# A linear-attention and maxout-FFN kernel: another hand-made order for its 1478 steps

## The chip, the cores and the metric

The kernel runs on one core of a Trainium2 chip. The metric is the device time in microseconds of one execution; the time of the kernel before is the median of three runs. The five engines are called as the profile calls them: PE (matrix products), DVE (vector), ACT (activation), POOL (GpSimd) and SP (here a queue of DMA issues alone).

## The reference

```python
def phi(x):                                   # x: 8 x 8 x 576 x 64, w_phi: 64 x 128
    proj = np.einsum('bhsd,df->bhsf', x, w_phi)
    proj = proj - np.max(np.abs(proj), axis=-1, keepdims=True)
    return np.concatenate([np.exp(proj), np.exp(-proj)], axis=-1)
q_p, k_p = (phi(q), phi(k))
kv = np.einsum('bhsf,bhsd->bhfd', k_p, v)
z = np.sum(k_p, axis=2)
num = np.einsum('bhsf,bhfd->bhsd', q_p, kv)
den = np.einsum('bhsf,bhf->bhs', q_p, z)[..., None] + 1e-06
x = (num / den).transpose(0, 2, 1, 3).reshape(4608, 512)
h = np.maximum(np.maximum(x @ w1, x @ w2), x @ w3)   # w1..w3: 512 x 768
out = h @ w_out                                      # 768 x 512, out: 4608 x 512, float32
```

So there are 64 heads of linear attention, and behind them a feed-forward network (FFN) with a maximum of three branches over 4608 tokens.

## The kernel before

**Attention** goes in 16 units of four heads (two units to a batch). A unit loads Q, K and V; casts Q and K to bf16; transposes them (on PE with `tps` for units 0 to 3, with a DMA transpose on SP for the others); projects them (`psq`, `psk`, line 536); takes the maxima on DVE (`mqp`, `mk`, 555); takes the exponentials of K on ACT (`Ek`, 549); turns the maxima of Q and puts them into the transposed Q (`mT`, 567 and 571); projects Q again with the maxima taken off (`psm`, 615) and takes its exponentials (`Eq`, 628); weights V on POOL (`vab`, 590); forms K'V on PE (`kvps`, 644, copied to `kv_sb`, 649); and multiplies (`psn`, 662: four groups of ten products to a unit). DVE divides (`rden`, `x_sb`, 668 and 669), and the result goes transposed into `xT`: over PE for units 0 and 1 (`pxT`, 682), with a DMA transpose on SP for the others (692). This last transfer is called X.

**The FFN** goes in nine chunks of 512 tokens. Chunk 0 to 7 is the first 512 tokens of a batch and needs X of two units; chunk 8 is the 64 last tokens of all batches, put together by POOL (`x_last`, 832). A chunk has 12 products `up` of four matmuls each (`ups`, 715), taken up by ACT or DVE (`hT`, 721 to 725), and then four output tiles: a "straight" product of four matmuls (742), a "down" product of six onto it (747), a copy (`osb`, 755) and two stores (762). The branches are computed as differences to the first one, whose own part is the straight product; for that the weights are combined once at the start (`hT` copies at 802, `pm`, 813). The last tile of chunk 8 is cut into pieces of 256, 128 and 128 columns.

In the first matmuls of an `up`, two read the channels of the even unit and two those of the odd one.

**Order.** Every step is a closure ("node") with a number. A table `PLAN` lists all 1478 of them; each word gives the node, the engine (T for PE, D, A, G for POOL, S for SP), the buffer slots and a start, and `plan` takes them in that order:

```python
n, slots = nodes[int(what[:at])], iter(what[at + 1:])
n.eng, n.start = {"T": "PE", "D": "DVE", "A": "ACT", "G": "POOL", "S": "SP"}[what[at]], float(start)
for b in n.bufs:
    if b.index is None:
        b.index = int(next(slots), 36)
order.append(n)
```

The starts are planned values and no measurement. An engine carries out its instructions in the order in which they come, and waits where an operand or a buffer is not ready. `fill` puts spare matmuls (`idler`, 844) where the table leaves PE idle for long. Weights are loaded on POOL's queue (422), Q, K and V of most units on SP's (475). V of units 1 to 3 is held back by a copy of one element on DVE, the gate (473): the load waits until the copy has written into its buffer.

Of the kernel before, what the change touches and what calls it, by code (L numbers as in the profile page):

```python
# [96 lines left out]
0G@0.72 10S0@0.73 2D0@0.85 3D@1.07 6S0@1.19 1G@1.29 4A@1.30 8S@1.65 86G0@1.79 13S@2.11 15S1@2.57 85G@2.64 1076G@3.49 12D1@3.63  # L97
159G2@4.29 7A@4.38 9A@5.12 158G@5.14 16T1@5.15 5D@5.55 1079G@5.99 17D0@6.25 22T002300@7.02 27T45@7.26 25D@7.51 29A@7.74 26D@8.11
14A@8.45 31D@8.72 24A@9.07 18T6@9.22 23A@9.58 20T7@9.67 19D@9.92 228G1@10.03 28A@10.07 30D@10.54 37T12@10.69 32T36@10.92
21D@11.14 39A@11.17 93T5@11.25 40D@11.37 42T47@11.52 33A@11.66 45D@11.97 91T1@12.12 44A@12.15 35D@12.31 34A@12.49 89T4@12.57  # L100
94D1@12.92 38A@12.98 61T30@13.07 90D@13.27 43A@13.47 64T5@13.55 63A@13.81 92D@13.89 66A@14.30 46D@14.51 95T114111@14.66
65A@14.80 36D@14.85 47A0@15.29 1090T7@15.32 41D@15.46 62A@15.54 50G0@15.69 1086T5@15.92 48G@15.97 98D@16.06 1091A0@16.17
105T62@16.61 1087D@16.77 110T30@16.85 49G@17.09 51A@17.12 58T4@17.18 112A@17.37 113D@17.38 1088T7@17.66 59A@17.91 108D@17.99
52G@18.20 67T5@18.26 111A@18.39 1089D@18.59 162T3@18.74 60A@18.88 164T6@19.19 114D@19.20 53G@19.32 68A@19.37 55T7@19.64
69A@19.73 165D2@19.89 54A@20.07 115T04@20.21 57A@20.37 119D@20.58 70T056@20.66 56A@20.87 118D@20.92 87D0@21.26 117A@21.36
163D@21.36 88S@21.51 183T000700@21.70 116A@21.72 361S1@21.97 109D@21.98 71A@22.06 166T3@22.13 362S1@22.43 184A@22.46 167D@22.59
100T45@22.61 72D@22.81 124A1@22.95 77T30@22.96 104D@23.19 107A@23.20 127G1@23.35 1094T6@23.44 227G@23.63 97A@23.69 103D@23.80
106A@24.18 78D0@24.40 185A@24.67 1098T4@24.74 99D@25.02 102A@25.16 187D@25.63 1095A@25.65 131T21@26.04 96A@26.15 126G@26.16
160D2@26.24 186D@26.34 161S@26.49 173T37@26.62 133A@26.77 168T61@26.85 176D@27.10 1092T0@27.18 101A@27.26 125G@27.28 177D@27.71
120A@27.75 169A@28.00 1099D@28.32 123G@28.40 128T3@28.48 132A@28.49 122G@28.68 229D3@28.93 79T5@28.96 175A@28.97 171D@29.03  # L110
75T4@29.28 170A@29.46 1096T2@29.60 80D1@29.63 121G@29.79 174A@29.95 76D0@30.25 129A@30.44 172D@30.87 73T6@30.90 1077G@30.91
130A@30.95 137T5@31.22 1093A@31.43 1097D@31.48 365G0@31.71 143T141@31.80 138A@31.95 74D1@32.09 139A@32.46 1078G@32.83
188T73@32.84 178T02@32.96 145A@33.09 192D@33.21 140T6@33.28 144A@33.49 231T5@33.52 182D@33.55 364G@33.63 141A@33.89 134T1@33.97
181D@34.15 196A0@34.30 81T4@34.45 142A@34.55 197G0@34.75 191D@34.76 135A@34.89 148T61@35.04 232D0@35.10 152T0@35.36 189A@35.38
146T7@35.68 136A@35.72 149D0@35.72 83T5@36.00 180A@36.20 147D1@36.34 150T1@36.35 82A@36.69 198G@36.84 151D0@36.96 190A@37.34
153D1@37.58 233T6@37.66 179A@37.68 154T7@38.11 199A@38.17 84A@38.32 234D@38.36 193T4@38.42 156T1@38.48 242T110311@38.89
# [759 lines left out]
```

## Time and profile before

| what | value |
|---|---|
| median of three runs | 285.19 us (284.92 to 285.64) |
| the profiled execution's own time | 284.83 us |
| its span in the profile | 283.0 us (1.8 us lie around it) |
| clock of PE granted | 1.00 |
| PE busy | 273.1 us, 96% |
| DVE, ACT, POOL busy | 74%, 69%, 42% |
| first `up` of chunk 0 | at 41.58 us |
| DMA | 51.45 MB, mean 182 GB/s |

Times in rows of the profile are microseconds from the start of the span. In a timeline row stand start, duration of the group, engine, line, operation, output and inputs, count, and in square brackets the idle time of the engine ahead of it with what ended it ("issue": nothing that the profile shows). In a row of waits stand the engine and line, what was waited for, the sum, the count and the longest. In the chain stand start, length and what. In a row of windows stand the window, its length, the busy time of PE, PE's weight loads, DVE, ACT and POOL with their counts, the granted clock, the share of the DMA engines and GB/s.

### The profile page before, as it was taken

The page shows a single profiled execution, that of the slowest core. Times are in us where ns is not written, and L with a number is a line of the kernel's source. Part 1 is how long each engine was busy: PE and PEld are TensorE (multiplying, and loading weights), DVE is VectorE, ACT ScalarE, POOL GpSimd, SP SyncE. Part 2 cuts the span into 40 slices and gives each one's busy share as a digit, 9 for nine tenths or more (in the row PEclk, how much of TensorE's full clock was granted, in tenths as well). Part 3 has the DMA queues.
Part 4 walks back from the last instruction along what each step waited for, and adds up shares of the span by engine and source line. Part 5 has one row for each costly group of instructions (what it writes and reads, how often), then busy time and mean ns, then how long its engine had stood idle before and what let it go on. Part 6 is the DMA issues. An engine that isn't in the chain of part 4 may idle for free.

```text
span 283.0 us, 8534 instructions
## 1 busy us (share of the span) xinstructions
PE 273.1 (96%) x3524; PEld 154.1 (54%) x3563; DVE 208.9 (74%) x441; ACT 195.4 (69%) x447; POOL 117.8 (42%) x107
## 2 busy tenths in 40 slices
PE   8899989999999989999999999999999999999995
PEld 3476764565556635665556465555555455444443
DVE  4799988999887978879879759995886664055232
ACT  2799988898888869897886798887634762230120
POOL 8064787856390836722638609051114600000000
PEclk9999999999999999999999999999999999999999
DMA  7999999999989999999998469969706106050164
GB/s 185 245 207 237 255 172 270 315 213 192 357 328 194 201 271 325 163 241 211 245 299 150 94 188 249 182 123 206 205 1 123 41 2 130 0 109 5 37 145 155
DMA packets 68337, 51.45 MB, mean 182 GB/s; under 512 B 48778, under 2 KB 53066, under 8 KB 68298
## 3 DMA queue, kind: packets, MB, share of 16 engines
q1 hardware_dynamic: 63534, 45.28, 67.5%
q0 software_dynamic: 4000, 4.92, 10.2%
q10 hardware_dynamic: 764, 0.71, 0.7%
q8 instruction: 28, 0.46, 0.6%
q14 instruction: 11, 0.09, 0.1%
HBM read 34.64 MB, written 9.44 MB: 156 GB/s over the span
## 4 chain that ended last, share of the span: by engine, by line
PE 83%; DMA 9%; DVE 5%; issue 1%; POOL 1%; ACT 1%; POOLq 0%
PE ups L715 33%; PE ops L747 14%; PE ops L742 10%; PE psn L662 7%; DMA xT<-x_sb 5%; PE kvps L644 5%; PE psm L615 5%; PE psq L536 5%; DMA qk_bf<-in_q_dram 3%; PE pm L813 2%; DVE mqp L555 1%; DVE mk L555 1%; PE tps L498 1%; DVE qkT L501 1%; DVE x_sb L669 1%
## 5 line engine op out<-in xcount | busy, mean ns | idle before, releaser
L715 PE MATMUL ups<-xT,w_bf 128*128 128x512 bf16 x416 | 100.3, 379 | 2.1 <-DMA xT<-x_sb 1.2
L549 ACT ACTIVATE Ek<-psk 128x512 bf16<-128x512 f32 (+1 forms) x160 | 82.8, 571 | 16.8 <-PE psk L536 13.5
L628 ACT ACTIVATE Eq<-psm 128x512 bf16<-128x512 f32 (+1 forms) x160 | 78.8, 570 | 11.4 <-PE psm L615 10.7
L590 POOL TENSOR_TENSOR vab<-v_raw,em 128x1152 bf16<-128x1152 f32 (+1 forms) x36 | 68.0, 1906 | 44.4 <-ACT em L586 31.7
L715 PEld LDWEIGHTS <-w_bf 128*128 128x128 bf16 x432 | 40.6, 98 | 47.7 <-issue 2.3
L555 DVE TENSOR_REDUCE mqp<-psq 128x4 bf16<-128x512 f32 (+1 forms) x80 | 48.9, 632 | 8.3 <-PE psk L536 6.7
L555 DVE TENSOR_REDUCE mk<-psk 128x4 f32<-128x512 f32 (+1 forms) x80 | 49.0, 628 | 2.9 <-ACT Ek L549 2.1
L747 PE MATMUL ops<-wout_bf,hT 128*128 128x512 bf16 (+2 forms) x216 | 49.3, 367 | 0.6 <-issue 0.2
L721 DVE TENSOR_TENSOR hT<-hT,ups 128x512 bf16<-128x512 bf16 x54 | 36.0, 683 | 16.9 <-PE ups L715 15.2
L747 PEld LDWEIGHTS <-hT 128*128 128x128 bf16 x228 | 21.2, 98 | 22.0
L669 DVE TENSOR_TENSOR x_sb<-psn,rden 128x320 bf16<-128x320 f32 x64 | 31.5, 492 | 2.2
L723 ACT ACTIVATE hT<-ups 128x512 bf16<-128x512 f32 x33 | 19.4, 601 | 19.4 <-PE ups L715 19.3
L662 PEld LDWEIGHTS <-Eq 128*128 128x128 bf16 x640 | 25.2, 97 | 7.8
L725 DVE TENSOR_SCALAR hT<-ups 128x512 bf16<-128x512 f32 x21 | 14.3, 687 | 19.7 <-PE ups L715 19.5
L755 ACT COPY osb<-ops 128x512 f32<-128x512 f32 (+2 forms) x20 | 11.0, 553 | 25.6 <-PE ops L747 15.4
L662 PE MATMUL psn<-kv_sb,Eq 128*128 128x65 bf16 x640 | 27.2, 194 | 0.1
L536 PE MATMUL psq<-w,qkT 64*128 64x128 bf16 x288 | 24.3, 217 | 0.5 <-DVE qkT L501 0.5
L742 PE MATMUL ops<-xT 128*128 128x512 bf16 x88 | 23.9, 380 | 0.4
L536 PE MATMUL psk<-w,qkT 64*128 64x128 bf16 x288 | 24.1, 217 | 0.0
L536 PEld LDWEIGHTS <-qkT 64*128 64x128 bf16 x576 | 16.5, 94 | 12.5 <-issue 9.6
L481 POOL CAST qk_bf<-k_raw 128x1152 bf16<-128x1152 f32 x12 | 13.8, 1146 | 19.9 <-DMA k_raw<-in_k_dram 9.1
L615 PE MATMUL psm<-qkT,wphi_m 128*128 128x512 bf16 (+1 forms) x70 | 21.5, 358 | 0.0
(75 smaller groups left out, 235.7 us busy)
## 6 DMA issues: line engine op xcount, KB each, us to landing
v_raw<-in_v_dram SPq DMA_DIRECT2D x16, 576.0 KB
out_dram<-osb SPq DMA_DIRECT2D x65, 128.0 KB
q_raw<-in_q_dram SPq DMA_DIRECT2D x12, 576.0 KB
k_raw<-in_k_dram SPq DMA_DIRECT2D x12, 576.0 KB
w_bf<-in_moe_w_dram POOLq DMA_DIRECT2D x3, 768.0 KB, 8.2
qk_bf<-in_k_dram POOLq DMA_DIRECT2D x3, 288.0 KB, 13.2
qk_bf<-in_q_dram POOLq DMA_DIRECT2D x3, 288.0 KB, 9.5
wout_bf<-in_moe_w_out_dram POOLq DMA_DIRECT2D x1, 768.0 KB, 17.0
```

The lines of the kernel that those rows point to most:

```text
L536: nc.tensor.matmul(ps()[:, i, :], lhsT=cols[r, :], rhs=w2[r, c, :], start=True, stop=True)
L549: nc.scalar.activation(Ek[s]()[:, tiles_of(t0, n), :], of(1), EXP, scale=1.0 - 2.0 * s)
L555: nc.vector.tensor_reduce((mq, mk)[c]()[:, tiles_of(t0, n)], of(c), AXX, ALU.max, apply_absolute_value=True)
L590: (nc.vector if n_.eng == "DVE" else nc.gpsimd).tensor_tensor(vab()[:, g, t0:t1, 0:D], vb()[:, t0:t1, :], em()[:, g, t0:t1].unsqueeze(2).t ...
L615: nc.tensor.matmul(psm()[:, 0:w], lhsT=wphi_m, rhs=rhs, start=True, stop=True)
L628: nc.scalar.activation(Eqb()[s][:, cols], psm()[:, 0:w], EXP, scale=1.0 - 2.0 * s)
L662: nc.tensor.matmul(psn()[:, c, :], lhsT=Eqb()[g][:, t0:t0 + P], rhs=kv()[:, pr, ab, g, :], start=(g == 0), stop=(g == 1))
L669: nc.vector.tensor_tensor(x_sb()[:, pr, :, ab, :], psn()[:, :, 0:D], rden().to_broadcast([P, 5, D]), ALU.mult)
L715: nc.tensor.matmul(ups(), lhsT=w_bf[i + 1][:, ct, j * P:(j + 1) * P], rhs=tokens_of(ct), start=(ct == 0), stop=(ct == CT - 1))
L721: nc.vector.tensor_tensor(hT()[:, j, :], hT()[:, j, :], ups(), ALU.max)
L742: nc.tensor.matmul(ops_()[:, 0:width], lhsT=tile_of(ct, tt), rhs=line_w[c_i > MOVE][:, ct, cols], start=(ct == 0), stop=False)
L747: nc.tensor.matmul(ops_()[:, 0:width], lhsT=hT()[:, j, tt * P:(tt + 1) * P], rhs=wout_bf[:, j, cols], start=False, stop=(j == JT - 1))
```

## The change

Another `PLAN`, with the same 1478 nodes. Buffers, stages and all other code stay. 84 nodes go to another engine (most are copies out of PSUM between DVE and ACT), the others only to another place or slot. There are 7128 PE rows and 27 idlers in both. The table has 154 lines now, 155 before, so each later line of code has a number lower by one.

```diff
 PLAN = """
...
-353D0@92.97 439A@92.98 419T5@93.35 458A0@93.47 581D@93.59 1171T@93.67 360S@93.74 459A@93.74 420D1@94.19 579A@94.44 576D@94.81
-438A@94.93 1178T1@94.97 754G2@95.02 425S@95.24 1172A3@95.42 575D@95.42 567T75@95.93 578A@96.03 624G1@96.14 562T43@96.17
...
+352T6@92.10 1168A0@92.20 420D1@92.29 577T112511@92.51 572T14@92.75 353D0@92.91 425S@93.06 354T7@93.07 463G@93.11 573A@93.23
+689G2@93.39 1170T3@93.39 355D1@93.64 574A@93.74 579A@94.23 1171T@94.26 576D@94.38 461G@94.51 360S@94.56 578A@94.74 581D@95.38
...
 """
```

Here node 425, X of unit 5, stands behind node 360, X of unit 4, in the old rows and ahead of it in the new ones.

Three places. First PE at the end of attention: `psn` is the last group of unit 15, whose result SP then transposes, `ops` are output tiles of chunk 6, and `ups` is the first `up` of chunk 7. Before:

```order
L662 MATMUL psn_5299<-kv_sb_5224,Eq1_1_78 128x65
...
L742 MATMUL ops_5315<-w0_bf_81,xT_85 128x512 [waits DVE_49]
...
L747 MATMUL ops_5315<-wout_bf_84,hT_4986 128x512
...
L747 MATMUL ops_5280<-wout_bf_84,hT_4986 128x512
...
L742 MATMUL ops_5338<-w0_bf_81,xT_85 128x512
...
L747 MATMUL ops_5338<-wout_bf_84,hT_4986 128x512
...
L715 LDWEIGHTS w1_bf_82 [waits DMAHW1_49,DVE_49]
L715 MATMUL ups_5352<-xT_85,w1_bf_82 128x512 [waits PE_49]
...
L715 MATMUL ups_5352<-xT_85,w1_bf_82 128x512 [waits DMAHW4_49]
```

and now, again from the last `psn` of the unit:

```order
L661 MATMUL psn_5310<-kv_sb_5236,Eq1_0_76 128x65
...
L741 MATMUL ops_5321<-w0_bf_81,xT_85 128x512
...
L746 MATMUL ops_5119<-wout_bf_84,hT_4988 128x512
...
L746 MATMUL ops_5321<-wout_bf_84,hT_4988 128x512
...
L714 LDWEIGHTS w1_bf_82 [waits DMAHW3_49,DVE_49]
L714 MATMUL ups_5345<-xT_85,w1_bf_82 128x512 [waits PE_49]
...
L714 MATMUL ups_5345<-xT_85,w1_bf_82 128x512 [waits DMAHW4_49]
```

Each `ops` of line 742 stands for four matmuls and each of line 747 for six: 26 lay between `psn` and `ups`, now 16. The blocks taken away stand ahead of the `psn` now. The third matmul of the `up`, the first that needs unit 15, has a wait for its transfer in both.

Second DVE at some 18 to 22 us, where the gate of V of unit 1 (line 473, then 472) stands among maxima, `hT` copies of the weights and `qkT` copies. Before:

```order
L555 TENSOR_REDUCE mqp1_80<-psq_376 128x4
L802 COPY hT_374<-pwT_413 128x1024 [waits PE_49]
L555 TENSOR_REDUCE mk_467<-psk_389 128x4 [waits Activation_49]
L501 COPY qkT_482<-tps_450 128x1024 [waits PE_49]
L555 TENSOR_REDUCE mk_467<-psk_487 128x2 [waits PE_49]
L555 TENSOR_REDUCE mqp1_80<-psq_485 128x2
L473 CAST v_raw_569<-qkT_160 1x1 [waits DVE_49]
L501 COPY qkT_482<-tps_432 128x1024
```

and now:

```order
L554 TENSOR_REDUCE mqp1_80<-psq_391 128x4 [waits PE_49]
L554 TENSOR_REDUCE mqp1_80<-psq_404 128x4 [waits PE_49]
L472 CAST v_raw_459<-qkT_157 1x1 [waits DVE_49]
L801 COPY hT_387<-pwT_416 128x1024 [waits PE_49]
L500 COPY qkT_473<-tps_442 128x1024 [waits PE_49]
L500 COPY qkT_473<-tps_464 128x2x128 [waits PE_49]
L554 TENSOR_REDUCE mk_502<-psk_406 128x4 [waits Activation_49]
```

The gate moved ahead of the last `hT` copy and of the `qkT` copies behind it; SP's loads of V of unit 1 and of K of unit 5 follow it.

Third DVE ahead of chunk 2, the divisions of units 4 and 5. Before, `x_sb_2231` is unit 4 and `x_sb_2144` unit 5:

```order
L669 TENSOR_TENSOR x_sb_2144<-psn_2204,rden_2242 128x5x64 [waits DVE_49]
L668 RECIPROCAL rden_2247<-psn_2215 128x5 [waits PE_49]
L669 TENSOR_TENSOR x_sb_2231<-psn_2215,rden_2247 128x5x64 [waits DVE_49]
...
L669 TENSOR_TENSOR x_sb_2231<-psn_2273,rden_2299 128x5x64 [waits DVE_49]
L668 RECIPROCAL rden_2311<-psn_2288 128x5 [waits PE_49]
L669 TENSOR_TENSOR x_sb_2231<-psn_2288,rden_2311 128x5x64 [waits DVE_49]
...
L669 TENSOR_TENSOR x_sb_2144<-psn_2315,rden_2338 128x5x64 [waits DVE_49]
```

and now, with `x_sb_2246` for unit 4 and `x_sb_2168` for unit 5:

```order
L668 TENSOR_TENSOR x_sb_2168<-psn_2208,rden_2231 128x5x64 [waits DVE_49]
...
L668 TENSOR_TENSOR x_sb_2246<-psn_2219,rden_2251 128x5x64 [waits DVE_49]
L667 RECIPROCAL rden_2281<-psn_2254 128x5 [waits PE_49]
L668 TENSOR_TENSOR x_sb_2168<-psn_2254,rden_2281 128x5x64 [waits DVE_49]
L667 RECIPROCAL rden_2304<-psn_2268 128x5 [waits PE_49]
L668 TENSOR_TENSOR x_sb_2246<-psn_2268,rden_2304 128x5x64 [waits DVE_49]
...
L668 TENSOR_TENSOR x_sb_2246<-psn_2308,rden_2329 128x5x64 [waits DVE_49]
```

Unit 5's last division stood last of all and is now ahead of two of unit 4's; SP issues X of unit 5 first.

293 lines of the change are left out of this document (146 added, 147 removed).

## The prediction

> **What bounds the kernel now.** I read the page's first parts, then the waits of TensorE (PE), then the chain that ended last, and last the timelines around each wait. The page:
>
> ```profile
> span 283.0 us, 8534 instructions
> PE 273.1 (96%) x3524; PEld 154.1 (54%) x3563; DVE 208.9 (74%) x441; ACT 195.4 (69%) x447; POOL 117.8 (42%) x107
> PEclk9999999999999999999999999999999999999999
> ```
>
> PE is busy for 273.1 of 283.0 us at the full clock all along. The change keeps every matmul, so only the 9.9 us in which PE is not busy can be won, and part of those (start, last store) no order removes. Who makes PE wait:
>
> ```profile
> PE ups L715 <- DMA xT<-x_sb: 1.2, 2, 1.1
> PE idler L844 <- DVE idle L415: 1.0, 1, 1.0
> PE tps L498 <- issue: 0.7, 1, 0.7
> PE tps L498 <- DMA qk_bf<-in_q_dram: 0.7, 1, 0.7
> PE psq L536 <- DVE qkT L501: 0.5, 1, 0.5
> ...
> PE ops L747 <- issue: 0.2, 1, 0.2
> ```
>
> The only row that lies behind the first 42 us is the first: the FFN's first product waits for the transposed attention output (X below, `xT<-x_sb`). The chain, with start and length of each piece, has it three times, each X followed by the matmul that it holds:
>
> ```profile
> 97.15 5.18 DMA xT<-x_sb
> 102.37 0.59 PE ups L715 x2
> ...
> 153.11 5.43 DMA xT<-x_sb
> 158.59 2.32 PE ups L715 x10
> ...
> 189.12 4.60 DMA xT<-x_sb
> 193.76 4.04 PE ups L715 x18
> ```
>
> These are the X of units 5, 9 and 11, ahead of chunks 2, 4 and 5. In a chunk's first `up` two matmuls need the even unit and two the odd one, so each wait stands in front of the third matmul. When that was due:
>
> ```profile
> 49.62 1.73 PE ups L715 x8
> 234.15 0.62 PE psn L662 x20
> 100.69 0.61 PE L715 MATMUL ups<-xT,w_bf 128*128 128x512 bf16 x2
> 157.82 0.61 PE L715 MATMUL ups<-xT,w_bf 128*128 128x512 bf16 x2
> 193.26 1.95 PE L715 MATMUL ups<-xT,w_bf 128*128 128x512 bf16 x7
> ```
>
> Eight take 1.73, so one is 0.216 and two are 0.43. The third was due at 101.12, 158.25 and 193.69 and began at 102.37, 158.59 and 193.76: waits of 1.25, 0.34 and 0.07, together **1.66**. That is all that an order can win after the first `up`. Twenty `psn` (`L662`) take 0.62; the row is used below.
>
> **The change part by part.** Nothing is added or removed; 1478 steps get other places, and 84 of them another engine. I go by the places where the trace waits and where the new order takes cover away.
>
> *Chunk 2, X of unit 5.* Unit 5's last `psn` now comes ahead of unit 4's last, and SP issues X of unit 5 first. Between that `psn` and the first `up` there were 124 PE matmuls and are now 165. The added ones are two sets of 10 `psn` (0.31 each), one block of four wide ones (4 x 0.216 = 0.86), 16 small projections and a turn: 1.5 of cover more without the small ones, against a wait of 1.25. The wait goes: **-1.25**. Next late is X of unit 4, now second in SP's queue, whose cover falls from 138 matmuls to 128; it is needed by the first matmul of the `up`. I bound it at 0 to +0.3 and take 0.
>
> *Chunk 7, X of unit 15.* Here the new order takes two blocks away (see the PE rows shown with the change): 16 matmuls stand between the last `psn` and the `up`, before 26.
>
> ```profile
> 235.47 0.79 PE L662 MATMUL psn<-kv_sb,Eq 128*128 128x65 bf16 x20
> 236.84 0.49 DVE L669 TENSOR_TENSOR x_sb<-psn,rden 128x320 bf16<-128x320 f32 x1
> 237.36 1.33 SPq L692 DMA_TRANSPOSE xT<-x_sb  x1
> 240.89 0.40 POOL L832 COPY x_last<-xT 128x256 bf16<-128x256 bf16 x1 [16.21 <-DMA xT<-x_sb]
> 241.71 0.59 PE L715 MATMUL ups<-xT,w_bf 128*128 128x512 bf16 x2
> ```
>
> The last 10 `psn` began at 235.78 and left at 236.09, X was issued at 237.36 (1.27 later), and POOL's copy, which waits for X alone, began at 240.89: at most 3.53 for X, 4.80 after the `psn`. The cover is now 16 x 0.216 = 3.46 and two `up` matmuls, 0.43: 3.89. The third matmul waits 4.80 - 3.89 = **+0.9**; bounds 0.6 (POOL's own start taken off, X a little shorter) and 2.8 (X at 5.43). Before, it was covered: 0.82 passed between copy and `up`. The matmuls taken from here stand elsewhere and cost the same.
>
> *Chunks 4 and 5, X of units 9 and 11.* Between their last `psn` and the `up` there are now 125 matmuls instead of 129 (one block of four wide ones, 0.86, is gone) and instead of 126 (about 0.2 less). So these two stand no better than before. For unit 9:
>
> ```profile
> 150.00 1.10 PE L662 MATMUL psn<-kv_sb,Eq 128*128 128x65 bf16 x30
> 152.59 0.49 DVE L669 TENSOR_TENSOR x_sb<-psn,rden 128x320 bf16<-128x320 f32 x1
> ```
>
> Thirty `psn` at 0.031 end at 150.93; the `up` began 6.89 later, X was issued 2.18 later and landed 5.43 after that. With 0.86 less cover the third matmul is due 6.89 - 0.86 + 0.43 = 6.46 after the last `psn`. The landing is between 1.27 + 3.5 = 4.8 (division and transfer of unit 15, above) and 2.18 + 5.43 = 7.6. In the middle, 6.2, nobody waits; at the long end 1.15 are lost. For unit 11 the ends are much the same. I count the old waits (0.34 + 0.07) as gone and set **+0.3** for both together, bounds 0 and +2.3.
>
> *The pause in unit 3's transposes.* On the chain, 0.75 without a releaser:
>
> ```profile
> 36.74 0.86 PE L844 MATMUL idler<-idle 128*128 128x512 bf16 x2
> 37.53 0.30 PE L498 MATMUL tps<-ident,qk_bf 128*64 128x128 bf16 x4
> 38.58 0.53 PE L498 MATMUL tps<-ident,qk_bf 128*64 128x128 bf16 x12 [0.75 <-issue]
> ...
> q8 instruction: 28, 0.46, 0.6%
> ```
>
> No operand is missing there; 28 packets of instructions come over the queues, and one of them may be late here, while the transfers are dense. The new order has other rows at this point. Bounds 0 and -0.75. Of all the stretches of PE's program the waits name just one other with "issue" (0.2), so such a pause is rare, and I take it as gone: **-0.75**. The Trainium skill's "Runtime: NRT & Kernel Launch", section "Instruction fetch mechanics", says that a program is fetched in blocks of 256 instructions and that a crossing is mostly hidden. By that rule the crossing stands behind the same number of instructions in the new order, which has as many in all, and meets the same dense transfers: the pause comes again, the term is 0, and the median 0.75 higher. The trace has the pause once among many crossings, so it does not decide between the two.
>
> *The first 42 us.* Here raw loads move. On SP, V of unit 1 and everything behind it waits for a small copy on DVE (`L473`); that now stands ahead of the third `hT` copy, and the loads come beside the output weights, which POOL issued at 5.70:
>
> ```profile
> 2.59 19.74 SPq L475 DMA_DIRECT2D v_raw<-in_v_dram  x2
> 19.34 0.68 DVE L802 COPY hT<-pwT 128x1024 bf16<-128x1024 bf16 x1
> 23.71 1.46 PE L813 MATMUL pm<-wout_bf,hT 128*128 128x512 bf16 x5
> wout_bf<-in_moe_w_out_dram POOLq DMA_DIRECT2D x1, 768.0 KB, 17.0
> 8.00:10.00 2.00, 2.00 (x27) 1.08 (x22) 1.84 (x3) 1.60 (x4) 0.00 (x0) 1.00 1.12 289
> 18.00:20.00 2.00, 2.00 (x52) 1.77 (x49) 2.00 (x5) 2.00 (x7) 2.00 (x2) 1.00 1.24 207
> ```
>
> SP's second V went out at 21.9 (2.59 to 22.33 holds both); the weights landed at 5.70 + 17.0 = 22.7, and the first `pm`, which needs them, began at 23.71. At 18 to 20 us POOL's queue alone moves 207 GB/s (last column), at 8 to 10, with SP's loads beside it, both move 289. If V now starts at 19.4, some 2.5 earlier, and takes half of 289, the weights get 145 instead of 207 and lose 2.5 x 0.3 = 0.75, up to 1.3 with K of unit 5 behind it. The slack is 1.0: 0 to +0.3 of wait. Both loads of unit 3 move behind the others, several raw loads are bunched, and the DVE's chain between 14 and 21 us is sorted anew. The waits of the second block (0.7, 0.5) bound what can be won here, 1.2, and as much again what can be lost. I set **+0.3**, bounds -0.8 and +1.6.
>
> *Later loads.* Raw loads go out earlier than before, seven in a row on SP; the row of maxima of unit 3 goes on ACT's queue behind them. POOL was busy 42% and its casts wait less: hidden by the 96% of PE. **+0.15**, bounds 0 and +0.8. The engine swaps (`t1`, `kv`, `osb` between DVE and ACT) cost nothing: 74% and 69% busy, with PE between; without that cover 0.1 each.
>
> *The end.* The last piece is now 256 wide instead of 128:
>
> ```profile
> 279.39 0.37 ACT L755 COPY osb<-ops 128x256 f32<-128x256 f32 x1 [5.53 <-PE ops L747]
> 279.95 0.27 ACT L755 COPY osb<-ops 128x128 f32<-128x128 f32 x1 [0.18 <-PE ops L747]
> 280.24 0.34 ACTq L762 DMA_DIRECT2D out_dram<-osb  x1
> ```
>
> The copy is 0.10 longer, and twice the bytes leave behind it. From 280.24 to the end of the span 2.8 pass, of which the transfer is a part; bounds +0.1 and +0.6, taken **+0.3**.
>
> Sum: -1.25 - 0.41 + 0.3 + 0.9 - 0.75 + 0.3 + 0.15 + 0.3 = **-0.46**. The span goes from 283.0 to 282.5, the profiled execution from 284.83 to 284.4. The median of the runs, 285.19, stands 0.36 above that execution, so the median becomes 284.7. Most of what the change wins at chunk 2 it gives back at chunk 7.
>
> **The rivals.** Differences under 0.3% (0.86 us) cannot be told from none here.
>
> *A, the waits only change place* (above): 284.7. For it speaks that the cover at chunk 7 can be counted in matmuls, as can that at chunk 2.
>
> *B, faster: the reordered first 42 us gain instead of lose, and X of units 9 and 11 come in time.* The terms +0.3 (first 42 us), +0.3 and +0.15 become -0.4, 0 and 0: 284.7 - 1.15 = 283.6. For it: the rows of waits in the first 42 us add up to nearly 3 us, and the ends of the X transfers are spread. Against it: a moved load cannot land before the bytes ahead of it.
>
> *C, slower: the output weights are late.* If SP's loads get two thirds of 289 GB/s instead of half, the 207 x 3 us = 0.62 MB that are left go at 96 GB/s and land at 19.7 + 6.5 = 26.2, which is 2.5 behind 23.71; PE, which goes in order, loses that less what it can take first. The sum holds 0.3 of it already, so it decides, against 285.19 + 0.86, from a landing of about 25.4 on. Time: 284.7 + 2.5 - 0.3 = 286.9. For it: up to three loads lie beside the last part of the weights. Against it: equal shares give 0.3. The Trainium skill's "DMA: Bandwidth & Descriptors", section "Queues, rings and completion order", says that a DMA engine takes turns between its queues packet by packet. By that rule every load moved beside the weights takes its turn from them, and the queue with the larger packets gets the larger share, which speaks against this change; no row here shows the shares.
>
> *D, slower: X is long again.* With 5.43 at unit 9 and about 5.2 at unit 11, chunks 4 and 5 wait 1.15 and about 0.9; with 0.3 counted that is 284.7 + 1.75 = 286.45. Beyond 286.05 it comes from some 5.2 us on at both. The rows show 5.18, 5.43 and 4.60 there, against 3.53 with quiet queues at the end; fewer loads stand beside them now, since these moved forward.
>
> *E, nothing moves*: X of unit 5 is late for another reason (one late DMA engine) and waits again: +1.25 on A, 286.0. The 1.5 of added cover speak against it.
>
> **How the numbers follow.** A has 0.48, B 0.32, C, D and E 0.07, 0.08 and 0.05. A's own range is 283.9 to 285.6. With B and the low bound of the first 42 us the low end is 283.3; up to the near edges of C and D the high end is 286.2. Faster by over 0.3% (under 284.3): B, and the low tenth of A, together 0.36. Slower (over 286.05): C, D, and half of E, with the top of A 0.19. Same: the rest, 0.45.
>
> **What would show it.** Right: no wait for X at chunk 2, one of 0.6 to 1.2 in front of the third matmul of chunk 7's first `up`; the first `up` within 1 us of 41.6; no PE row with "issue" of 0.7; PE's last row followed by a 256-wide copy. Wrong: a wait at chunk 2 or above 1 at chunk 4 or 5; a first `pm` after 25; a first `up` at 40 or before. The sum is wrong above all if the first 42 us, the term with the widest bounds, come out beyond them.

## The result, and the profile after

| | before | changed |
|---|---|---|
| median of 20 runs each | 285.26 us (284.05 to 287.85) | 289.01 us (286.88 to 296.97) |
| profiled execution, its span | 284.83, 283.0 us | 287.33, 285.5 us |

The changed kernel takes 1.0114 times as long, 95% interval 1.0088 to 1.0140: it is slower. The forecast was 284.7, with 286.2 as the high end, and slower had 0.19. The profiled executions differ by 2.5 us, the medians by 3.75. Medians here and below are of all runs; ratios leave out runs that lie more than 1.5% above the fastest of the same kernel, here four of the changed one.

The page of the changed kernel, its head, PE and the rows of the clock and the DMA engines:

```profile
span 285.5 us, 8573 instructions
...
PE 274.8 (96%) x3563; PEld 154.0 (54%) x3563; DVE 210.1 (74%) x439; ACT 195.5 (68%) x451; POOL 115.4 (40%) x106
...
PEclk9999999999999999999999999999999999999999
DMA  7999999999998999999999329698312314240334
```

PE does the same work (39 records fewer were kept before, which may be why its busy time reads 1.7 lower there). Who makes PE wait now (engine and line, what was waited for, sum, count, longest):

```profile
PE ups L714 <- DMA xT<-x_sb: 3.2, 4, 1.5
PE idler L843 <- DVE idle L414: 1.0, 1, 1.0
PE psm L614 <- DMA qkT<-mT: 0.7, 1, 0.7
```

The FFN's wait for X rose from 1.2 to 3.2, a wait of unit 15's `psm` for its maxima came in, and the row with "issue" in `tps` is gone. In the chain that ended last (start, length, what) stand the transfers that hold PE, each with its follower:

```profile
96.35 5.08 DMA xT<-x_sb
101.47 1.90 PE ups L714 x8
...
153.75 5.83 DMA xT<-x_sb
159.62 4.04 PE ups L714 x18
...
223.34 3.21 DMA qkT<-mT
226.59 0.70 PE psm L614 x3
...
239.69 3.35 DMA xT<-x_sb
243.08 1.46 PE ups L714 x6
```

These are X of unit 4 (chunk 2; the forecast had X of unit 5 there), X of unit 9 (chunk 4), the maxima of unit 15, and X of unit 15 (chunk 7). At chunk 4 the two X come one behind the other, and PE waits for both (the first stands in front of the first matmul, the second in front of the third):

```profile
157.90 0.61 PE L714 MATMUL ups<-xT,w_bf 128*128 128x512 bf16 x2 [0.24 <-DMA xT<-x_sb]
159.62 1.67 PE L714 MATMUL ups<-xT,w_bf 128*128 128x512 bf16 x7 [1.11 <-DMA xT<-x_sb]
```

To see what each place costs, I compared the times in both traces at points where PE has done the same matmuls (at the two `up` rows, all but a few):

| point | before | changed | changed minus before | step since the row above |
|---|---|---|---|---|
| `kvps` of unit 6, in chunk 1 | 97.44 | 96.68 | -0.76 | -0.76: the start, with the pause gone |
| chunk 2's first `up` | 100.69 | 101.47 | +0.78 | +1.54: X of unit 4 late |
| a straight product of chunk 3 | 154.73 | 154.50 | -0.23 | -1.01: X of unit 5 no longer late, less small pieces |
| chunk 4's first `up` | 157.82 | 157.90 | +0.08 | +0.31: X of unit 8 late |
| projections of unit 12 | 175.72 | 176.75 | +1.03 | +0.95: X of unit 9 late |
| a `psn` of unit 11 | 186.70 | 187.57 | +0.88 | -0.15 |
| chunk 8's second-last straight piece | 278.10 | 280.33 | +2.23 | +1.35: unit 15, its maxima and its X |
| end of the span | 283.0 | 285.5 | +2.5 | +0.27: the wider last piece |

So the start won 0.8 us, and chunk 2 (+0.5 net), chunk 4 (+1.3) and unit 15 (+1.35) gave it back four times over.

Why is X of unit 4 late? SP's queue at chunk 2, the changed kernel (start, duration of the issue, line, operation):

```profile
89.46 1.10 SPq L761 DMA_DIRECT2D out_dram<-osb  x2
90.67 4.22 SPq L512 DMA_TRANSPOSE qkT<-qk_bf  x1
94.94 2.99 SPq L691 DMA_TRANSPOSE xT<-x_sb  x2
```

and before:

```profile
90.73 4.08 SPq L513 DMA_TRANSPOSE qkT<-qk_bf  x1
94.90 3.63 SPq L692 DMA_TRANSPOSE xT<-x_sb  x2
```

SP spends 4 us on the issue of T7, the transpose of unit 7's Q and K, and is free at 94.9 in both. In the changed kernel unit 5's last division ended at 92.69 and unit 4's at 94.03:

```profile
92.19 0.49 DVE L668 TENSOR_TENSOR x_sb<-psn,rden 128x320 bf16<-128x320 f32 x1
93.53 0.49 DVE L668 TENSOR_TENSOR x_sb<-psn,rden 128x320 bf16<-128x320 f32 x1
```

Yet the two X went out at 94.94 and 96.35. X of unit 4 left 2.3 after its division: 0.9 of it SP was still at T7, and 1.4 it took the issue of X of unit 5. In both kernels the X that goes out second lands last. Before, the second one was unit 5's, which the third matmul needs (97.15 to 102.33: wait 1.25). Now it is unit 4's, which the first matmul needs, two matmuls (0.43) earlier (96.35 to 101.43: wait 1.63). No run changes the order of these two X alone; the nearest is the kernel with the new start and the old rows here, below, where they wait 0.6 and 0.6.

The medians differ by 1.2 us more than the two traces. The profiled execution of the changed kernel is the third fastest of its 20, and its start was a good one: its first `up`, at 40.33, is the earliest in the 13 traces that have the new start (40.33 to 42.72; the seven with the old one 41.21 to 42.91). In 8 of the 20 runs PE's mean granted clock is 0.992 to 0.994, and the profiled run had none of that. But the kernel before has a mean of 0.994 or less in 24 of the 108 runs that stand beside the experiments. The 12 changed runs without it have a median of 288.39, the 84 others of the kernel before one of 285.24. So the clock can account for some 0.6 us of the 3.75, by this estimate, and not for the rest.

### The profile page after: what moved, and what is told of

Same layout as the page of the kernel before. It is cut to its first block, busy times and chain, and to the rows that moved or that the text cites. A ratio compares the mean times of both kernels' runs of the same rounds, so it can differ in the third digit from the quotient of the medians.

```text
span 285.5 us, 8573 instructions
## 1 busy us (share of the span) xinstructions
PE 274.8 (96%) x3563; PEld 154.0 (54%) x3563; DVE 210.1 (74%) x439; ACT 195.5 (68%) x451; POOL 115.4 (40%) x106
## 4 chain that ended last, share of the span: by engine, by line
PE 75%; DMA 14%; DVE 5%; ACT 3%; POOL 1%; issue 1%; POOLq 0%; SPq 0%; ACTq 0%; DVEq 0%
PE ups L714 31%; PE ops L746 12%; PE ops L741 9%; PE psn L661 5%; DMA xT<-x_sb 5%; PE psm L614 5%; PE kvps L643 5%; DMA qkT<-qk_bf 4%; PE psq L535 4%; DMA qk_bf<-in_k_dram 3%; PE pm L812 1%; DVE mqp L554 1%; ACT Ek L548 1%; DMA qkT<-mT 1%; DVE mk L554 1%; DVE x_sb L668 1%
## 5 line engine op out<-in xcount | busy, mean ns | idle before, releaser
L714 PE MATMUL ups<-xT,w_bf 128*128 128x512 bf16 x432 | 101.5, 379 | 3.2 <-DMA xT<-x_sb 3.2
L746 PE MATMUL ops<-wout_bf,hT 128*128 128x512 bf16 (+2 forms) x228 | 51.9, 368 | 0.0
L722 ACT ACTIVATE hT<-ups 128x512 bf16<-128x512 f32 x27 | 16.3, 603 | 30.3 <-PE ups L714 30.2
L754 ACT COPY osb<-ops 128x512 f32<-128x512 f32 (+2 forms) x23 | 12.8, 568 | 23.3 <-PE ops L746 23.2
L661 PE MATMUL psn<-kv_sb,Eq 128*128 128x65 bf16 x640 | 26.6, 194 | 0.4 <-ACT Eq L627 0.4
L741 PE MATMUL ops<-xT 128*128 128x512 bf16 x96 | 24.7, 379 | 0.0
L724 DVE TENSOR_SCALAR hT<-ups 128x512 bf16<-128x512 f32 x27 | 18.5, 685 | 7.5 <-PE ups L714 7.3
L754 DVE COPY osb<-ops 128x512 f32<-128x512 f32 (+1 forms) x15 | 9.9, 661 | 17.6 <-PE ops L746 14.6
```

What stands on the lines that cost most here:

```text
L661: nc.tensor.matmul(psn()[:, c, :], lhsT=Eqb()[g][:, t0:t0 + P], rhs=kv()[:, pr, ab, g, :], start=(g == 0), stop=(g == 1))
L714: nc.tensor.matmul(ups(), lhsT=w_bf[i + 1][:, ct, j * P:(j + 1) * P], rhs=tokens_of(ct), start=(ct == 0), stop=(ct == CT - 1))
L741: nc.tensor.matmul(ops_()[:, 0:width], lhsT=tile_of(ct, tt), rhs=line_w[c_i > MOVE][:, ct, cols], start=(ct == 0), stop=False)
L746: nc.tensor.matmul(ops_()[:, 0:width], lhsT=hT()[:, j, tt * P:(tt + 1) * P], rhs=wout_bf[:, j, cols], start=False, stop=(j == JT - 1))
```

## The experiments

A hybrid takes the rows of one table up to a start and those of the other behind it. Ratios are to the kernel before, in runs made beside them; its medians there were 285.1 to 286.0. In the diffs of single steps only the moved steps are shown; buffer slots of later steps change with some of them.

**Four stretches, one at a time.** The new rows for the start, for chunks 1 and 2, for 3 and 4, and for the end, the old ones elsewhere. The joint of the first:

```diff
 386D@57.69 429G1@57.71 277A@57.71 301S2@57.86
+491S0@58.0 384A@58.0 276A@58.0 494G0@58.0
```

The words without a sign are the last new ones; those with a plus are the first old ones, which stood from 57.59 on in their own table. The diffs of the other hybrids are to be read alike.

> The new order up to the middle of chunk 0 (PE start 58 us in the table), the old order from there on. In the trace of the changed kernel PE is 0.95 us ahead at that point. Theory 'thin cover' (the loss sits where transfers have less PE work in front of them, all of it later): -0.5 to -1.2 us against before. Rival 'bunched loads' (the raw loads brought forward in the first 60 us lengthen the transfers after them, wherever they are covered): +0.5 us or more, and longer X transfers than in the kernel before.

> The new order from the middle of chunk 0 to the middle of chunk 2 (58 to 117 us), the old one around it. Trace of the changed kernel: the wait for X of unit 5 (1.25) goes, one for X of unit 4 (1.6) comes, PE loses 0.6 in this stretch. Thin cover: 0 to +1.0 us, with PE's wait at the first matmul of chunk 2's up instead of the third. Bunched loads: the same wait, and +1 or more behind it, since loads are brought forward here too.

> The new order from the middle of chunk 2 to chunk 4 (117 to 174 us), the old one around it. Trace of the changed kernel: PE waits 0.4 for X of unit 8 and 1.3 for X of unit 9, against 0.3 before, and loses 1.3 in this stretch. Thin cover: +0.8 to +1.8 us, with these two waits. Bunched loads: near 0, since the loads that stand beside these transfers were brought forward in earlier stretches, which are old here.

> The new order from chunk 4 (174 us) to the end, the old one ahead of it. Trace of the changed kernel: waits of 0.85 for the maxima row of unit 15 and 0.6 for X of unit 15, and 0.3 more behind the last matmul; PE loses 1.3 in this stretch. Thin cover: +1.2 to +2.0 us with these two waits. Bunched loads: only the end and X of unit 15, +0.5 to +0.9.

Measured: 290.43 (ratio 1.0170, 1.0125 to 1.0215), 297.01 (1.0408, 1.0359 to 1.0457), 296.69 (1.0410, 1.0357 to 1.0462), 293.88 (1.0289, 1.0228 to 1.0350). The four excesses add up to far more than the change costs, and PE's largest waits say why: in the first one of 2.8 up to 76 us for X of unit 3, which went out 3.9 after its division, and in the second, third and fourth:

```profile
PE psq L536 <- DVE x_sb L669: 4.6, 1, 4.6
```

```profile
PE psn L662 <- DVE x_sb L669: 7.4, 1, 7.4
```

```profile
PE ops L742 <- DVE x_sb L669: 4.9, 1, 4.9
```

These waits are in neither kernel. At a joint one engine is handed work earlier than its fellow, and stalls until the queues are in step. The runs do not split the change; they are artefacts of the cut. The later hybrids were cut where nearly all steps ahead are the same in both tables.

**The start alone.** New rows up to 37.06, old ones (from 36.35) behind:

```diff
 149D1@36.38 135A@36.43 180A@36.91 153D0@37.0
+229D3@37.06 364G@37.06 189A@37.06 150T3@37.06
```

> New order for the first 36 us of PE's table alone, the old one behind it; other place of the joint than e1, so that no engine finds its queue out of step there. Thin cover: about -1.0 us against before (PE is about 1 us ahead there in the trace of the changed kernel, the pause of 0.75 in unit 3's transposes gone), and the old waits for X of units 5, 9 and 11. Rival 'bunched loads': no faster than before, with longer X transfers.

Measured: 283.91 (282.94 to 285.06, 12 runs), ratio 0.9941 (0.9909 to 0.9972), faster than both kernels. Its first `up` stands at 40.80 against 41.58 before. The wait for X in its trace:

```profile
PE ups L715 <- DMA xT<-x_sb: 0.9, 2, 0.5
```

It is chunk 2 alone, with X of unit 4 and of unit 5 late by 0.6 each; chunk 4 does not wait. PE is 0.78 ahead of before at chunk 1's first `up` (0.73 in the changed kernel; a little less than the expectations took from its trace). Rival 'bunched loads' expected no gain here. So the start is a gain of 0.6%, and all behind it costs 1.0114/0.9941, or 1.7%.

**The rest alone.** Old rows up to 36.35, new ones (from 37.06) behind:

```diff
 149D0@35.72 83T5@36.0 180A@36.2 147D1@36.34
+198G@36.35 199A@36.35 179A@36.35 153D1@36.35
```

> Old order for the first 36 us, the changed kernel's behind it: the counterpart of e5. If the start's gain is its own and adds up: 1.2 to 2.0 us above the changed kernel, about 290.5, with the pause in unit 3's transposes and, in some runs, a granted clock of 0.994. If the gain in the start is eaten by later waits: the same as the changed kernel within 0.5.

Measured: 292.76 (288.26 to 293.57), ratio 1.0145 (1.0073 to 1.0218, from three of its six runs). It has a joint wait of 2.15 at 45 us, and X of unit 4 late by 1.85, of unit 8 by 1.92 and of unit 9 by 0.53; the pause in unit 3's transposes is not in its trace. With the run before it, 0.9941 x 1.0145 = 1.0085, which does not contradict the whole change of 1.0114; with the joint wait in it and so wide an interval, it shows no more than that.

**New up to chunk 3, up to chunk 4, and from chunk 6 on.** The same cut at 150.57 (shown), at 174.27, and old rows up to 202.23 with new ones behind:

```diff
 681T3@149.93 613D1@150.11 679T5@150.25 889A@150.26
+1422G@150.57 1101G@150.57 950G@150.57 620S@150.57
```

> New order through chunk 3 (150 us), the old one behind it. It has the start and the exchange of X of units 4 and 5, not the late X of unit 8 nor the end. Thin cover: -0.9 to +0.3 us, with a wait of 1 to 1.7 for X of unit 4 and none above 0.5 for X of units 8 and 9. Bunched loads: +1 or more, since nearly all loads that move are in it.

> As before it, but through chunk 4 (174 us), so that X of units 8 and 9 are issued one right behind the other. Thin cover: 1.0 to 1.6 us more than e6, with waits of 0.4 and 1.3 at chunk 4. Bunched loads: the same as e6 within 0.4.

> Old order up to chunk 5 (202 us), the new one behind it: the late maxima row of unit 15, the 16 instead of 26 matmuls ahead of chunk 7, the wider last piece. Thin cover: +1.2 to +2.0 us, with waits of some 0.8 and 0.6 and 0.3 behind the last matmul. Bunched loads: at most +0.9, since no load moves behind 202 us.

Measured: 288.75 (ratio 1.0058, 1.0012 to 1.0104, from seven of its twelve runs; the trace is of one of 289.81), 291.29 (1.0197, 1.0135 to 1.0259) and 287.97 (1.0088, 1.0053 to 1.0123). The first two wait 2.15 and 1.82 for X of unit 4, and 2.45 and 1.80 for X of unit 8: unit 8's late `psn` is already in the first, so it does not isolate chunk 4, and the second has joint waits of 1.1 and 1.2. The third has the old pause (0.61), a joint wait of 1.14 at 216 us, and waits of 0.55 and 0.49 for unit 15. Its mean clock is 0.994, and its stretch at half clock stands behind no X (window, its length, busy PE, weight loads, DVE, ACT, POOL, then the granted clock, the share of the DMA engines, GB/s):

```profile
13.00:14.00 1.00, 1.00 (x11) 0.37 (x11) 0.60 (x2) 0.56 (x2) 0.00 (x0) 0.50 1.14 207
14.00:15.00 1.00, 1.00 (x22) 1.00 (x22) 0.62 (x2) 1.00 (x3) 0.00 (x0) 0.50 1.18 207
15.00:16.00 1.00, 1.00 (x17) 0.64 (x12) 0.20 (x1) 0.08 (x1) 0.00 (x0) 0.50 1.20 205
```

Three more traces (new rows in chunks 3 and 4, new rows at the end, and the old start with the rest new) have such a stretch there. So a mean clock of 0.994 does not say that a wait for X was behind it.

What stands firmer is a count over all traces with full stores: in eight of nine with the new rows at chunk 2, X of unit 4 is late by 1.3 to 2.2. With the old rows there, the two X together cost 0.9 to 1.8 (the run further down that delays them left out). So with the exchange the wait at chunk 2 does not go; in most traces it is longer.

**Chunk 4 mended.** In the new table unit 8's last `psn` (node 612) comes 4.6 us later than before. It goes back ahead of two blocks of chunk 3, with its division and its X:

```diff
-612T1@147.99 613D1@150.11 620S@150.88
+612T2@144.45 613D1@146.57 620S@147.34
```

> The changed kernel with one step moved back: unit 8's last group of psn 3.9 us (in the table) earlier, so that X of unit 8 goes out some 4 us ahead of X of unit 9 instead of right in front of it. Thin cover with the two transfers getting in each other's way: X of unit 8 takes about 4 us and X of unit 9 4 to 5 instead of 6.0 and 5.8, chunk 4's waits fall from 1.7 to 0.5 or less, and the median is 1.0 to 1.5 us below the changed kernel's 289.0. Rival 'bunched loads': X of unit 9 stays above 5.5, and the median within 0.4.

Measured: 288.82, ratio 1.0112 (1.0064 to 1.0160). At chunk 4 it did what it should: X of unit 8 took 3.45 instead of 6.02, X of unit 9 5.13 instead of 5.83, and the two waits fell from 1.68 to 0.50. The median did not move. This trace had no gain from the start (0.06 behind before at chunk 1's first `up`, where the changed kernel was 0.73 ahead), X of unit 4 was late by 2.24, and behind it PE's clock fell:

```profile
101.00:102.00 1.00, 0.00 (x0) 0.00 (x0) 1.00 (x3) 0.46 (x1) 0.00 (x0) 1.00 0.82 184
102.00:103.00 1.00, 0.35 (x1) 0.13 (x2) 1.00 (x3) 0.00 (x0) 0.00 (x0) 0.76 1.09 386
103.00:104.00 1.00, 1.00 (x4) 0.39 (x3) 0.43 (x1) 0.00 (x0) 0.00 (x0) 0.50 1.11 401
104.00:105.00 1.00, 1.00 (x4) 0.36 (x3) 0.00 (x0) 0.42 (x1) 0.69 (x1) 0.50 1.03 382
105.00:106.00 1.00, 1.00 (x4) 0.30 (x3) 0.00 (x0) 0.97 (x6) 0.83 (x2) 0.53 1.05 389
106.00:107.00 1.00, 1.00 (x6) 0.35 (x4) 0.75 (x2) 0.94 (x3) 1.00 (x1) 1.00 1.07 396
```

The clock is at a half for 0.48 + 1 + 1 + 0.94 = 3.4 us, which costs half of that, 1.7, on top of the wait; over the run the mean is 0.993. The other five runs of this kernel have means of 0.998 or more, so the clock is not what held its median; what did stays open. The Trainium skill's "TensorE: Matmul & The Clock Gate", Part 1, says that the clock is halved after an idle window of some 3.4 us, and that these windows run freely and do not start with the work. The 3.4 agrees; the wait that brought it was shorter than the page's window.

**The end mended.** Two blocks of chunk 6 back behind unit 15's last `psn`, and the `psm` of unit 15 two `up` products later:

```diff
-1061T40@223.51 1049T7@223.85 1073T3@232.78 1067T6@235.27
+1061T40@225.47 1049T7@225.59 1067T7@233.97 1073T3@233.65
```

> The changed kernel with two things moved back at the end: the two blocks of chunk 6 (10 matmuls, 2.2 us) stand behind unit 15's last psn again, and the first psm of unit 15 stands behind two up products. Thin cover: the waits of 0.85 for the maxima row and 0.6 for X of unit 15 go, the last matmul and the median are 1.0 to 1.5 us earlier. If only the wider last piece counts at the end: unchanged within 0.3.

Measured: 288.99, ratio 1.0120 (1.0072 to 1.0167). The wait for the maxima of unit 15 (0.85) is gone. X of unit 15 is still late by 0.47: its `psn` ends earlier, but the divisions still end late on DVE. From 185 to 270 us this trace loses 0.4 against before instead of 1.35. Against that the trace was 0.47 behind before at chunk 1's first `up`, X of unit 4 was late (2.18) and the clock fell (0.994, as in four of the six runs); the median shows nothing of the gain.

**Chunk 2: one load out of SP's way.** In the new table the load of Q of unit 15, needed 30 us later, stands ahead of T7:

```diff
-1011S0@86.67
+1011S0@101.0
```

> The changed kernel with one issue moved on SP: the load of Q of unit 15, which stands ahead of the transpose of unit 7 (T7) and is needed 30 us later, goes behind X of unit 4. Theory Q (SP's queue sets both X of chunk 2): T7 goes out 1.4 us earlier, X of unit 4 about 1.5 earlier, the wait at chunk 2 falls from 1.6-2.2 to 0.1-0.6, the half clock behind it goes too, and the median falls by 1.5 to 3 us from 289.0, to 286.0-287.5. Rival R (X itself is slow while loads run, or divisions are late): the wait stays at 1.4 or more and the median at 288.5 to 289.5.

Measured: 288.61 (286.97 to 290.64), ratio 1.0086 (1.0054 to 1.0119), which cannot be told from the changed kernel's. This trace runs some 2.4 us behind the changed kernel's from the first `up` on. Theory Q missed, and rival R had the wait and the median right; with the 2.4 taken off, the two X went out only 0.4 sooner:

```profile
84.44 5.36 SPq L512 DMA_TRANSPOSE qkT<-qk_bf  x1
89.90 3.22 SPq L761 DMA_DIRECT2D out_dram<-osb  x4
93.22 3.59 SPq L512 DMA_TRANSPOSE qkT<-qk_bf  x1
96.90 3.00 SPq L691 DMA_TRANSPOSE xT<-x_sb  x2
```

The four halves of stores that now stand alone took 3.22, where stores and load together had taken 3.88: of the load's issue of 1.40, 0.66 came free. X of unit 4 went out 1.9 after its division and took 5.39; the wait was 1.53. So taking an issue out need not free all its time.

**All three mended.**

```diff
-1011S0@86.67 612T1@147.99 1061T40@223.51 1049T7@223.85 1067T6@235.27
+1011S0@101.0 612T2@144.45 1061T40@225.47 1049T1@225.59 1067T1@233.97
```

> The changed kernel with three repairs together: the one of e13 at chunk 2, that of e9 at chunk 4 (unit 8's last psn back ahead) and that of e10 at the end. Theory P (chunk 2, chunk 4 and the end are the whole loss, on top of a start that wins 1): waits at chunk 2 and 4 together under 1.2 us, no wait for V of unit 15, no stretch at half clock, median 284.5 to 286.0, level with the kernel before or a little under. Rival: the loss comes from something spread over the program; then it stays at 287.5 or more although these waits are gone.

Measured: 288.33 (284.67 to 293.35), ratio 1.0056 (1.0019 to 1.0094). Better than the change, but not level with before. In this trace X of unit 4 took 3.80 and landed 0.3 before its `up`, so chunk 2 did not wait, though its rows there are those of the run before, which waited 1.53; at the end the maxima no longer waited. But chunk 4 waited 2.61 for X of unit 9:

```profile
145.32 6.26 SPq L512 DMA_TRANSPOSE qkT<-qk_bf  x1
151.68 1.37 SPq L691 DMA_TRANSPOSE xT<-x_sb  x1
153.09 0.65 SPq L474 DMA_DIRECT2D q_raw<-in_q_dram  x1
153.79 1.12 SPq L761 DMA_DIRECT2D out_dram<-osb  x2
155.01 2.57 SPq L691 DMA_TRANSPOSE xT<-x_sb  x1
```

Unit 8's division had ended at 147.68, 4.0 before its X went out: SP was held by a transpose whose issue took 6.26 here and 4.26 in the changed kernel. The rows around chunk 4 are those of the kernel with chunk 4 mended alone, where the same X was late by 0.50: one place waits 0.5 in one execution and 2.6 in another.

**Bytes or issues?** Each store of chunks 0 to 4 writes 4 rows instead of 64, as many issues, 4.9 MB less; on the new order and, as control, on the old:

```diff
                     for dram_ap, rows in pieces:
+                        if c_i < 5:
+                            dram_ap, rows = dram_ap[0:4], slice(rows.start, rows.start + 4)
                         queue_of[n_.eng].dma_start(dram_ap[..., cols], part()[rows, 0:width])
```

> The changed kernel; each store of chunks 0 to 4 writes 4 rows instead of 64, as many issues in the same places, about 4.9 MB less through the DMA engines between 70 and 200 us (these output rows are left out). Theory D (the DMA engines are full until 160 us in the new order, so X of units 4, 8 and 9 take 5 to 6 us instead of 3.5): these X take 3.5 to 4.5, the waits at chunks 2 and 4 together fall from 3.3 to under 1, the median from 289.0 to 285.5-287. Theory Q (the issues on SP alone set when X goes): the issue of T7 still takes 4 us, X of units 4 and 9 still 5 or more, waits together 2.5 or more, median 288-289.5.

> The kernel before with the same light stores, as the control of e17. Theory D: its waits at chunks 2, 4 and 5 (1.66 together) fall under 0.6, the median to 283.8-284.6, so e17 stands within 0.5 to 2.5 us of it instead of 3.7. Theory Q: 285 as before, and e17 3 to 4 us above it.

Measured: 286.20 (284.68 to 287.30), ratio 1.0018 (0.9992 to 1.0045), and 284.49 (283.05 to 285.85), ratio 0.9965 (0.9940 to 0.9990). The two orders stand 1.7 apart instead of 3.75. With light stores the new order has no wait at chunk 2, and at chunk 4 one of 0.78; the old one has 0.48 at chunk 4. PE's row in the new order:

```profile
PE ups L714 <- DMA xT<-x_sb: 1.0, 2, 0.6
```

T7's issue still took 3.95, but X of unit 4 went out 0.6 earlier and, issued at 95.74, was there when the `up` began at 99.9: at most 4.2 instead of 5.08. No run of the new order with light stores has a mean clock below 0.998 (two of the old order's have 0.993 and 0.994). So the traffic has a part in how long X takes and in half of what lies between the two orders. Theory D has the median and the waits right, but not every X: that of unit 9 still took 5.08 in the new order (before the cut of bytes 5.83) and 5.58 in the old one. Light stores do not remove the wait behind unit 15 (0.58), where the queues are quiet. One reservation: smaller stores also give SP and the `osb` buffers back sooner, and the two runs do not separate that.

The share of the DMA engines ahead of chunk 4 and behind it (the last three columns are clock, share and GB/s), before, changed, and changed with light stores:

```profile
140.00:160.00 20.00, 19.68 (x307) 11.38 (x302) 16.83 (x37) 15.63 (x39) 11.45 (x9) 1.00 0.88 207
160.00:180.00 20.00, 19.79 (x292) 11.33 (x294) 15.53 (x34) 16.94 (x40) 8.51 (x7) 1.00 0.76 183
```

```profile
140.00:160.00 20.00, 18.64 (x328) 11.14 (x329) 17.25 (x37) 14.80 (x35) 12.16 (x10) 1.00 1.02 240
160.00:180.00 20.00, 20.00 (x287) 11.18 (x286) 14.73 (x31) 17.44 (x40) 9.11 (x9) 1.00 0.58 134
```

```profile
140.00:160.00 20.00, 19.39 (x264) 10.76 (x257) 16.96 (x37) 15.41 (x37) 12.23 (x10) 1.00 0.77 177
```

The new table moves loads forward, so the engines are full up to 160 us (1.02 against 0.88) and emptier behind (0.58 against 0.76). X of unit 8 and 9 lie in the full stretch. That the loads, of all that moved, are what costs there is argued: the runs took bytes from stores and not from loads.

**A longer wait.** The start-alone kernel with two loads and a store ahead of both X of chunk 2:

```diff
-493S0@97.45 1169S@97.91 622S0@99.11
+493S0@94.41 1169S@94.42 622S0@94.43
```

> The kernel of e5 with a load, a store and another load put ahead of X of units 4 and 5 on SP: the same computation, both X go out some 2.7 us later. Theory H (a wait of PE of 2 us or more costs a stretch at half clock besides): PE waits about 3 to 4 us at chunk 2, then runs some 3 us at about half the granted clock, mean clock of the run .992 to .995, median 283.9 + 2.7 + 1.6 = 288.2 (287.5 to 289). Rival without that stretch: 286.6 (286 to 287) and the clock at .999.

Measured: 290.32 (289.26 to 290.63), ratio 1.0144 (1.0103 to 1.0186), 2 us above what theory H gave and 3.7 above its rival. The mean clock is 0.986 to 0.994 in every run. X of unit 4 went out 2.5 later and took 6.45 instead of 4.93, so PE waited 4.2; then the clock:

```profile
102.00:103.00 1.00, 0.00 (x0) 0.00 (x0) 0.18 (x1) 0.00 (x0) 0.00 (x0) 0.98 0.67 87
103.00:104.00 1.00, 0.00 (x0) 0.00 (x0) 0.00 (x0) 0.00 (x0) 0.00 (x0) 0.50 1.27 283
...
108.00:109.00 1.00, 1.00 (x4) 0.44 (x3) 0.33 (x1) 0.49 (x2) 1.00 (x1) 0.50 1.05 391
109.00:110.00 1.00, 1.00 (x5) 0.32 (x4) 0.96 (x2) 0.00 (x0) 1.00 (x2) 0.61 0.47 182
110.00:111.00 1.00, 1.00 (x7) 0.51 (x6) 0.76 (x2) 0.00 (x0) 1.00 (x1) 1.00 0.01 5
```

6.8 us at a half, two stretches of 3.4, where H had counted one. Against the start-alone trace PE is 4.0 behind at the `up` and 6.1 behind from 104 us of that trace on. Here the clock adds half as much again to the wait.

**Two attempts at a better kernel.** The start-alone kernel with unit 9's `psn` ahead of a block of chunk 3, and with T7 ahead of a store:

```diff
-1259T@147.33 679T1@148.63 677T3@148.95 681T0@149.27
+679T1@147.33 677T3@147.65 681T0@148.14 1259T@148.29
```

```diff
-1177S@89.18 496S2@90.38
+496S2@89.03 1177S@92.5
```

> e5 (new order for the first 36 us, old behind it) with one more step moved: unit 9's last three psn groups ahead of a block of 1.3 us that stood in front of them, so that X of unit 9 has that much more cover at chunk 4. Thin cover: e5's wait at chunk 4 (0.2 to 0.4) goes, 0 to 0.4 us below e5, that is about 283.7 and 0.6% below the kernel before. Rival: DVE, which works off the divisions one by one, sets when X of unit 9 goes out; then nothing changes.

> The kernel of e5 (new start, old rest) with one store on SP put behind the transpose of unit 7 instead of ahead of it. Theory Q: T7 goes out some 2.5 us earlier, X of units 4 and 5 at 94.2 and 95.6 instead of 95.4 and 96.8, the two waits of chunk 2 (.58 and .64) fall to 0-0.4 together, median 283.0 (282.6 to 283.4). Rival: the store waits between T7 and X as long as before, or another row comes last: 283.9 as e5.

Measured: 285.63, ratio 0.9988 (0.9961 to 1.0016), and 284.71 (283.05 to 287.85), ratio 0.9964 (0.9930 to 0.9998). Neither beats the start alone. The first has no wait for X of unit 9, but its `psn` waits 0.62 for `Eq` and the projections 1.15 for `osb` on DVE. In the second T7 went out at 89.39 instead of 92.23 and X of unit 4 came in time, but X of unit 5 still went out at 97.02 (X of unit 4 took 2.36 to issue) and was late by 1.27: the two waits of 0.6 became one.

## Why the prediction was wrong, point by point

**Chunk 2 failed, and it is the largest error.** The step was: "Next late is X of unit 4, now second in SP's queue, whose cover falls from 138 matmuls to 128; it is needed by the first matmul of the `up`. I bound it at 0 to +0.3 and take 0." It counted PE's matmuls behind the last `psn`, as if X left when the division ended. X leaves when SP is free, and T7's issue held SP until 94.9 in both kernels. The row for this was in the trace of before. What was taken as -1.25 is +0.5 in the profiles (+1.54 for X of unit 4, -1.01 behind it), and with the stretch at half clock behind it up to 1.7 more in the runs that have one. Of the 3 us between the forecast span and the profiled one this place makes 1.8, chunks 4 and 5 make 1.2 and unit 15 makes 0.45; the start and the loads give 0.45 back. That X of unit 5 would come in time was right; it was no gain, as the exchange gave the second place to the X that is needed earlier. Two of the prediction's own signs of being wrong came: a wait at chunk 2 (1.63) and one above 1 at chunk 4 (1.29). Rival E had X late here, but for the wrong unit. That SP's queue decides, and not the count of matmuls, is read from the traces; of the runs that moved T7 or a load ahead of it one shifted the wait to X of unit 5, and with the load moved chunk 2 waited 1.53 in one trace and not at all in another.

**Chunks 4 and 5: mis-sized.** Taken -0.41 + 0.3; the trace has +0.31 up to chunk 4's first `up` and +0.95 behind it, and nothing at chunk 5. The matmuls were counted behind unit 9's `psn`; that unit 8's last `psn` had moved 4.6 us back (161 matmuls ahead of the `up` instead of 205), so that its X now runs right ahead of unit 9's (6.02 and 5.83), was not looked at. The bound of 2.3 held it. With unit 8 forward again, the waits are 0.50 in one trace; with all three places mended, that X went out late behind a transpose all the same, and the wait was 2.61. So the nearness of the two X is one cause here and not the only one.

**Later loads: priced at the wrong place.** They were put at +0.15, with POOL's shorter waits hidden by PE. What the runs show is a price in X: the engines' share ahead of chunk 4 rose from 0.88 to 1.02, and with 4.9 MB of stores taken away 2 of the 3.75 us between the orders go. Rival D had X of unit 9 late by 1.15 (measured 1.29) and held against itself that fewer loads would stand beside it; the engines were fuller there, not emptier.

**Unit 15: right, and incomplete.** X of unit 15 was to wait 0.9 and waited 0.58 (issue to landing 3.35, forecast at most 3.53). The wait for its maxima in front of `psm`, 0.85, was not foreseen; the same cut of cover acts one step earlier. Together +1.35 in the trace.

**The first 42 us: right in sign only with the pause.** The pause was taken as -0.75 and the rest as +0.3; together they are -0.76, so the rest came to nothing in these two traces. The sum called this the term with the widest bounds; it is not the one that failed. The first `pm` stood at 22.80 and not after 25: rival C's late weights did not come. The first `up` stood at 40.33, somewhat outside the 1 us around 41.6: the first half of rival B came in, its second, X of unit 9 in time, did not. The pause in unit 3's transposes is in none of the 13 profiles that have the new start, and in six of the seven with the old; so the other reading that the term weighed, that the pause would come again behind the same number of instructions, is not what the traces show. It was worked out from the blocks of 256 instructions of the Trainium skill's "Runtime: NRT & Kernel Launch", section "Instruction fetch mechanics"; whether the pause is such a fetch at all, no run shows. In medians the start is worth 1.7 us (ratio 0.9941), more than the 0.8 at chunk 1 in these traces.

**The end was right:** +0.27, forecast +0.3, with a 256-wide last copy:

```profile
282.18 0.37 ACT L754 COPY osb<-ops 128x256 f32<-128x256 f32 x1 [1.06 <-PE ops L746]
```

**The clock was missing altogether.** The sum priced a wait at its length, while some runs show 3.4 us at half clock behind one. It is not what made the forecast fail: the changed runs without such a stretch still have a median of 288.39. Open: why the median stands 1 us above the profiled execution even so; the traces show X of unit 4 late by anything from 0 to 2.2 with the new rows at chunk 2.

## What to carry to other kernels

In these traces a transfer started only when its issuing queue was free, so count its lead from the end of the issue ahead of it and not from the end of the work that feeds it; where two transfers stand in line, an exchange only chooses which is late, and the first needed should go first. Price loads that are moved forward at the transfers that they then lie beside, and look at all transfers in that stretch, not only at the one that waited before. Where PE waits over 2 us, allow for 1.7 more for the clock: three of seven waits of 2.1 to 2.8 us had such a stretch behind them.

## What the runs showed of the hardware

- Behind a wait of PE the granted clock can fall to a half for 3.4 us or a multiple of it. Of seven waits of 2.1 to 2.8 us three had one such stretch behind them and four had none (2.14, 2.15, 2.45 and 2.61); all four waits of 4.2 us and more had two or three; none of the shorter ones after 33 us had any. Four traces have a stretch at 13 to 16 us, ahead of any X.
- An X alone in its stretch takes 3.3 to 3.5 us (unit 15, in every trace). Between 90 and 160 us it takes 3.4 to 6.7, and with the same rows around it other times in other executions (X of unit 4: 3.80 with all three mended, 5.39 with the load alone moved).
- SP is held 2.4 to 7.9 us by the issue of one transpose of Q and K, and 1.3 to 4.4 by that of one X.
